# One ScalarE transfer per output tile in place of four from the sync engine, in a linear-attention and two-MoE kernel

## The chip, the cores and the metric

The kernel runs on one core of one Trainium2 chip. The metric is the time of one execution on the device in microseconds (us). The profile is one execution recorded by the hardware profiler; its engines are TensorE (PE, with its weight loads as PEld), VectorE (DVE), ScalarE (ACT), GpSimd (POOL) and the sync engine (SP), which issues transfers and computes nothing.

## The reference

Three stages follow one another. The change lies at the very end of the third.

```python
def _attn_ref(q, k, v, alpha):            # 4 batches, 8 heads, 768 steps, head size 48
    for t in range(S):
        state = alpha[:, :, t, :, None] * state + np.einsum('bhd,bhe->bhde', k[:, :, t], v[:, :, t])
        y[:, :, t] = np.einsum('bhd,bhde->bhe', q[:, :, t], state)

def _moe_ref(x, w_in, w_out, a, b):       # 3072 tokens, 384 -> 2048 -> 384
    h = x @ w_in
    P = a[0] + a[1] * h + a[2] * h**2 + a[3] * h**3
    Q = 1.0 + np.abs(b[0]) * np.abs(h) + np.abs(b[1]) * h**2
    return (P / (Q + 1e-06)) @ w_out

def _moe2_ref(x, w_in, w_out, g_ln):      # 3072 tokens, 384 -> 1024 -> 384
    h = x @ w_in
    solu = h * softmax(h)
    ln = (solu - mean(solu)) / np.sqrt(var(solu) + 1e-06) * g_ln
    return ln @ w_out
```

The result has 3072 rows (batch by step) of 384 float32 numbers.

## The kernel before, in words

The steps are cut into six chunks (NCH) of 128, and a chunk holds 4 batches by 128 steps, which is 512 tokens. Attention and the first MoE run over the chunks together; from about 500 us on only the end of the first MoE and the second MoE are left. The second MoE has 24 tiles `s` of 128 tokens, four to a chunk. The words "up tile" and "down tile" below stand for its two products.

- `n_up` (L696) makes the up product of one tile on PE: 18 matmuls of 512 columns into one of three PSUM buffers.
- `n_soft` and `n_norm` (L713, L730) do the softmax and the normalization, passing the tile between DVE and ACT several times (L722 max, L723 exponential, L726 product, L728 square, L736 and L737, L741), and L743 transposes it in blocks of 32 into a buffer shared by the four tiles of the chunk.
- `n_turn` (L748) runs when all four tiles of a chunk are there: 16 transfers (L753) on SP, each of 32 partitions by 1024 elements, regroup the blocks. A regrouped tile `qq` holds 32 steps of each of the four batches.
- `n_split` (L755) makes a high part on ACT (L758) and a low part (L759) on POOL, or on DVE for tiles 0 and 20. There are three slots of each.
- `n_down` (L762) makes the down product on PE, 24 matmuls of 384 columns into one of two PSUM buffers `op`.
- `n_out` (L773) copies `op` to an SBUF tile `o` on ACT (L776); `o` shares two buffers. Because the partitions of `o` are 4 batches by 32 steps, the tile goes to four separate blocks of the result, each contiguous; the loop at L778 issues one transfer for each from SP (L779), 32 partitions by 384 elements, 48 KB.

The loop at the end of `network` (L915 to L932) writes the tiles out: it splits up to three tiles ahead of the down product, and skips the down product after some up tiles, so that downs run some tiles behind the ups. The last eight down tiles, 16 to 23, come after the last up tile. Each engine executes its own instructions in order. The order on an engine isn't quite that of the program text: the tile framework is opened with `schedule_with_timeline_sim=True` (L1042), and a planner orders the instructions by simulated times, and inserts the waits. SP takes all transfers of the kernel in one such order, the L753 transfers of a later chunk and the L779 stores of earlier tiles among them.

After the stage a flag that was computed earlier decides whether a fallback is run (L1013 to L1016); it is not taken here, but its code holds the same functions.

Of the kernel before, what the change touches and what calls it, by code (L numbers as in the profile page):

```python
# [30 lines left out]
def kernel(  # L31
# [15 lines left out]
    nc = tc.nc  # L47
    nc.scalar.preload_act_table_set("natural_log_exp_and_others")
    B, H, S, D = q.shape
# [103 lines left out]
    def network(fast):  # L153
# [7 lines left out]
        if fast:  # L161
# [7 lines left out]
                out=ident, in_=ident, pattern=[[-1, 128]], compare_op=ALU.not_equal, fill=1.0, base=0, channel_multiplier=1  # L169
# [603 lines left out]
        def n_out(s, op):  # L773
            c, qq = divmod(s, 4)
            o = moe_pool.tile([128, DM], F32, name="o", tag="st", bufs=2)
            nc.scalar.activation(o, op, AF.Copy)  # L776
            to = out.rearrange("(b c q j) d -> c q b j d", b=B, c=NCH, q=4)[c, qq]
            for b in range(B):  # L778
                nc.sync.dma_start(out=to[b], in_=o[32 * b:32 * b + 32])  # L779

        def n_tile(s):
            n_up(s)
# [132 lines left out]
        for s in range(len(EARLY), NS):  # L915
            if s % B == 0 and 1 < s // B + 1 < NCH:
                _run(n_load(s // B + 1))
            n_tile(s)
            if s % B == B - 1:
                n_turn(s // B)  # L920
            while cut < min(done + AHEAD, (s + 1) // B * B):
                n_split(cut)
                cut += 1
            if s not in SKIP:
                n_out(done, n_down(done))
                done += 1
        while done < NS:
            while cut < min(done + AHEAD, NS):
                n_split(cut)
                cut += 1  # L930
            n_out(done, n_down(done))
            done += 1  # L932
# [114 lines left out]
```

## Time and profile before

| | us |
|---|---|
| median of 3 runs | 805.31 (801.63 to 811.93) |
| the profiled execution, its own time | 804.26 |
| its span, first to last instruction | 802.5 |
| mean granted TensorE clock in it | 0.955 of full speed |

The span covers what the engines recorded; 1.76 us of the execution's time lie outside it. Times in the rows below are counted from the start of the span. In a timeline row the first number is the start, the second the duration, both in us; "idle before" in brackets says how long the engine had waited and for what. The SPq rows are the sync engine's issues of transfers, merged where several follow one another.

### The profile page before, as it was taken

What the parts mean: (1) busy time and instruction counts of PE and PEld (TensorE: products, weight loads), DVE (VectorE), ACT (ScalarE), POOL (GpSimd) and SP (SyncE); (2) the same over time, 40 slices, a digit from 0 to 9 for tenths busy, and PEclk for the clock granted to TensorE, in tenths of its full rate; (3) what the DMA queues carried; (4) which work ended last, traced back from release to release, by engine and by line L of the source; (5) the groups of instructions that cost most, each with busy time, mean ns of one, the idle gap of its engine ahead of it and who ended that gap; (6) DMA issues with size and microseconds to landing.
All of it is one profiled execution on the core that took longest, in us unless ns stands there. A gap on an engine that the chain in (4) does not pass through costs nothing. (4 is left out here: it accounts for less than half of the span.)

```text
span 802.5 us, 13911 instructions
## 1 busy us (share of the span) xinstructions
PE 733.8 (91%) x4976; PEld 611.1 (76%) x4976; DVE 641.6 (80%) x1110; ACT 534.4 (67%) x983; POOL 363.8 (45%) x306
## 2 busy tenths in 40 slices
PE   4677787889999989999999999999999999999995
PEld 4565565667787868877777788888888989988994
DVE  6894998998999898979898976567877697877720
ACT  2224756678786878788887879788775555555531
POOL 3254757777654554445454434243242524452331
PEclk9857798999999989999999999999999999999998
DMA  7778229362764476454827160460014454451552
GB/s 170 171 177 245 83 83 235 100 162 79 236 150 149 92 242 137 138 119 141 199 78 176 50 135 14 148 247 0 1 44 111 128 115 109 125 118 48 125 133 57
DMA packets 87279, 101.75 MB, mean 127 GB/s; under 512 B 34464, under 2 KB 63136, under 8 KB 87200
## 3 DMA queue, kind: packets, MB, share of 16 engines
q1 hardware_dynamic: 87200, 100.77, 47.6%
q8 instruction: 41, 0.67, 0.4%
q14 instruction: 38, 0.31, 0.1%
HBM read 60.59 MB, written 27.56 MB: 110 GB/s over the span
## 5 line engine op out<-in xcount | busy, mean ns | idle before, releaser
L583 PE MATMUL hp<-xt,g 128*128 128x512 f32 x864 | 229.0, 408 | 24.5 <-DVE p L614 19.9
L583 PEld LDWEIGHTS hp<-xt,g 128*128 128x128 f32 x864 | 165.3, 195 | 66.8 <-DVE p L614 25.3
L617 POOL TENSOR_TENSOR gl<-p,gh 128x512 fp32r<-128x512 f32 x96 | 130.5, 1359 | 187.3 <-ACT gh L616 114.5
L629 PE MATMUL x2p<-gh,g 128*128 128x512 f32 x576 | 196.5, 397 | 0.2 <-ACT gh L616 0.2
L629 PEld LDWEIGHTS x2p<-gh,g 128*128 128x128 f32 x576 | 109.8, 191 | 25.9 <-issue 0.6
L629 PE MATMUL x2p<-gl,g 128*128 128x512 f32 x288 | 113.6, 394 | 0.3 <-POOL gl L617 0.3
L767 PE MATMUL op<-w2oh,room 128*128 128x384 f32 x384 | 101.8, 339 | 0.2 <-DVEq L1014 0.2
L759 POOL TENSOR_TENSOR room<-room,room 128x1024 fp32r<-128x1024 f32 x22 | 53.7, 2445 | 103.0 <-ACT room L758 92.9
L612 DVE SCALAR_TENSOR_TENSOR w<-w,co,hp 128x512 f32<-128x512 f32 x84 | 62.0, 738 | 43.0 <-ACT hp L611 42.5
L703 PE MATMUL h<-w2ih,x 128*128 128x512 f32 x288 | 90.8, 395 | 0.0
L591 ACT ACTIVATE w<-ah,co 128x512 f32<-128x512 f32 x96 | 69.3, 721 | 7.1 <-DVE hp L613 6.9
L590 ACT ACTIVATE p<-hp,co 128x512 f32<-128x512 f32 x96 | 65.8, 685 | 12.2 <-POOL gl L617 11.7
L609 DVE SCALAR_TENSOR_TENSOR p<-p,co,hp 128x512 f32<-128x512 f32 x84 | 61.8, 735 | 14.1 <-ACT p L590 13.6
L616 ACT ACTIVATE gh<-p 128x512 fp32r<-128x512 f32 x96 | 59.9, 624 | 18.5 <-DVE p L614 8.0
L611 ACT ACTIVATE hp<-ah 128x512 f32<-128x512 f32 x84 | 50.1, 596 | 32.1 <-DVE p L609 31.5
L767 PEld LDWEIGHTS op<-w2oh,room 128*128 128x128 f32 x384 | 70.1, 188 | 1.6 <-DVEq L1014 0.5
L588 ACT ACTIVATE ah<-hp 128x512 f32<-128x512 f32 x96 | 56.5, 589 | 15.6 <-PE hp L583 15.4
L767 PE MATMUL op<-w2ol,room 128*128 128x384 f32 x192 | 65.1, 339 | 0.0
L629 PEld LDWEIGHTS x2p<-gl,g 128*128 128x128 f32 x288 | 54.4, 189 | 12.7 <-POOL gl L617 0.8
L703 PEld LDWEIGHTS h<-w2ih,x 128*128 128x128 f32 x288 | 53.9, 188 | 11.7
L614 DVE SCALAR_TENSOR_TENSOR p<-p,co,hp 128x512 f32<-128x512 f32 x84 | 62.0, 739 | 1.0
L610 ACT ACTIVATE ah<-w,co 128x512 f32<-128x512 f32 x84 | 60.5, 720 | 1.3
(165 smaller groups left out, 1280.4 us busy)
## 6 DMA issues: line engine op xcount, KB each, us to landing
room<-room SPq DMA_DIRECT2D x96, 128.0 KB, 2.3
qk_d<-qk SPq DMA_DIRECT2D x10, 771.0 KB, 4.5
st<-in_moe_w_in_dram SPq DMA_DIRECT2D x15, 512.0 KB, 5.2
st<-in_moe_w_out_dram SPq DMA_DIRECT2D x20, 384.0 KB, 3.8
qks<-qk_d SPq DMA_DIRECT2D x20, 257.0 KB, 5.6
x<-x_d SPq DMA_DIRECT2D x18, 256.0 KB, 3.4
out_dram<-o SPq DMA_DIRECT2D x96, 48.0 KB, 1.6
ra<-in_alpha_dram SPq DMA_DIRECT2D x44, 96.0 KB, 2.8
```

The costliest lines, as they stand in the source:

```text
L583: last["PE", u] = nc.tensor.matmul(hp, lhsT=w[:, kt, 128 * o:128 * o + 128], rhs=xts[c][:, kt, xx, :], start=(kt == 0 and w is hi and xx = ...
L590: nc.scalar.activation(p, hp, AF.Square, bias=co[:, 7:8])
L591: nc.scalar.activation(w, ah, AF.Square, bias=co[:, 6:7])
L609: nc.vector.scalar_tensor_tensor(p, p, a1, hp, ALU.add, ALU.mult)
L610: nc.scalar.activation(ah, w, AF.Ln, bias=rest)
L612: nc.vector.scalar_tensor_tensor(w, w, rest, hp, ALU.add, ALU.mult)
L614: fin[u] = nc.vector.scalar_tensor_tensor(p, p, a0, hp, ALU.add, ALU.mult)
L616: last["ACT", u] = nc.scalar.activation(gh, p, AF.Copy)
L617: last["POOL", u] = nc.gpsimd.tensor_tensor(gl, p, gh[:].bitcast(F32), ALU.subtract)
L629: nc.tensor.matmul(x2ps[c][d], lhsT=w[:, o, 128 * d:128 * d + 128], rhs=gg, start=(f == 0 and w is hi and gg is gh), stop=(f == NF1 - 1 an ...
L703: nc.tensor.matmul(hp[:, 512 * n:512 * n + 512], lhsT=x2s[c][:, kt, x, CH * b:CH * b + CH], rhs=w2[w][:, kt, 512 * n:512 * n + 512], start ...
L767: nc.tensor.matmul(op, lhsT=x[:, 128 * f:128 * f + 128], rhs=w2[w][:, f, :], start=(f == 0 and x is hi and w == "oh"), stop=(f == NF2 - 1 ...
```

## The change

The loop of four transfers over the batches is replaced by one transfer of the whole tile, 128 partitions by 384 elements (192 KB), with a destination of three dimensions (4 batches, 32 steps, 384). It is issued by ACT, the engine that makes `o`.

```diff
         def n_out(s, op):
             c, qq = divmod(s, 4)
             o = moe_pool.tile([128, DM], F32, name="o", tag="st", bufs=2)
             nc.scalar.activation(o, op, AF.Copy)
             to = out.rearrange("(b c q j) d -> c q b j d", b=B, c=NCH, q=4)[c, qq]
-            for b in range(B):
-                nc.sync.dma_start(out=to[b], in_=o[32 * b:32 * b + 32])
+            nc.scalar.dma_start(out=to, in_=o)
```

## Rows read from the trace of the kernel before

**Rows 1.** Page, busy time of each engine, with share of the span and instructions

```profile
PE 733.8 (91%) x4976; PEld 611.1 (76%) x4976; DVE 641.6 (80%) x1110; ACT 534.4 (67%) x983; POOL 363.8 (45%) x306
```

**Rows 2.** Stretches: length, then busy PE, PEld, DVE, ACT, POOL; clock, DMA share, GB/s

```profile
625.00:766.00 141.00, 141.00 (x708) 127.84 (x707) 107.25 (x220) 79.04 (x157) 54.98 (x27) 1.00 0.42 106
766.00:793.00 27.00, 26.69 (x149) 25.78 (x147) 3.76 (x6) 7.26 (x12) 7.18 (x4) 1.00 0.53 125
793.00:803.00 10.00, 0.00 (x0) 0.00 (x0) 0.00 (x0) 0.43 (x1) 0.00 (x0) 0.60 0.11 26
```

**Rows 3.** Waits from 755 us on: us in total, times, longest

```profile
ACT o L776 <- DMA out_dram<-o: 1.8, 2, 1.5
PEld op L767 <- DVEq L1014: 0.5, 1, 0.5
PEld op L767 <- ACT o L776: 0.3, 1, 0.3
```

**Rows 4.** Timeline of 762 to 786 us, without PE

```profile
763.43 0.47 ACT L776 ACTIVATE o<-op 128x384 f32<-128x384 f32 x1
...
763.93 5.13 SPq L779 DMA_DIRECT2D out_dram<-o  x8
...
764.12 1.15 ACT L728 ACTIVATE jk<-room,sm 128x1024 bf16<-128x1024 f32 x1 [0.22 <-DVE sm L727]
...
767.48 1.25 DVE L743 STREAM_TRANSPOSE room<-room 128x1024 f32<-128x1024 f32 x1
769.17 11.06 SPq L753 DMA_DIRECT2D room<-room  x16
...
773.41 1.06 ACT L758 ACTIVATE room<-room 128x1024 fp32r<-128x1024 f32 x1 [1.85 <-DMA room<-room]
774.51 1.22 DVE L759 TENSOR_TENSOR room<-room,room 128x1024 fp32r<-128x1024 f32 x1 [5.78 <-ACT room L758]
775.36 0.49 ACT L776 ACTIVATE o<-op 128x384 f32<-128x384 f32 x1 [0.88 <-PE op L767]
776.01 1.06 ACT L758 ACTIVATE room<-room 128x1024 fp32r<-128x1024 f32 x1 [0.17 <-DMA room<-room]
777.15 2.39 POOL L759 TENSOR_TENSOR room<-room,room 128x1024 fp32r<-128x1024 f32 x1 [11.15 <-ACT room L758]
...
780.33 5.63 SPq L779 DMA_DIRECT2D out_dram<-o  x12
```

**Rows 5.** Timeline of PE's weight loads where they waited

```profile
775.78 0.30 PEld L767 LDWEIGHTS op<-w2oh,room 128*128 128x128 f32 x2 [0.48 <-DVEq L1014]
...
784.11 0.19 PEld L767 LDWEIGHTS op<-w2oh,room 128*128 128x128 f32 x1 [0.26 <-ACT o L776]
```

**Rows 6.** SP's issues of three lines: duration min/median/max in ns, first and last start

```profile
L779 SPq DMA_DIRECT2D out_dram<-o x96: 314/419/1634, 631.4 to 796.0; - x96
...
L638 SPq DMA_DIRECT2D x_d<-x2e x12: 320/376/932, 198.2 to 624.4; - x12
...
L541 SPq DMA_DIRECT2D w2o_d<-st x8: 524/525/525, 306.5 to 430.0; - x8
```

**Rows 7.** Page, transfers: count, KB each, median us from issue to landing

```profile
room<-room SPq DMA_DIRECT2D x96, 128.0 KB, 2.3
...
out_dram<-o SPq DMA_DIRECT2D x96, 48.0 KB, 1.6
...
x_d<-x2e SPq DMA_DIRECT2D x6, 256.0 KB, 3.3
```

**Rows 8.** Timeline of ACT and SP at the end, and one 1 us stretch

```profile
792.94 0.49 ACT L776 ACTIVATE o<-op 128x384 f32<-128x384 f32 x1 [3.75 <-PEq L1014]
793.45 2.92 SPq L779 DMA_DIRECT2D out_dram<-o  x4
...
795.96 0.42 SPq L779 DMA_DIRECT2D out_dram<-o  x1
...
794.00:795.00 1.00, 0.00 (x0) 0.00 (x0) 0.00 (x0) 0.00 (x0) 0.00 (x0) 0.97 0.46 114
```

## The prediction, made before the run

> **What bounds the kernel now.** I read the views from the whole to the place of the change. The page's busy times come first: PE leads with 91% of the span, and DVE with 80% and ACT with 67% come behind [rows 1]. A share over the whole span says little about one stage, so the view of stretches is next. The stores start at 631 us [rows 6], so only the stretches from 625 us on matter. There PE is busy in all of 141 us up to 766, and in 26.69 of the 27 us up to 793, at the full granted clock; ACT is busy in 79.04 and 7.26 us of the same stretches, so 61.96 + 19.74 = 81.7 us of ACT are free [rows 2]. After 793 us only the last copy and the last stores are left, with the way out of the program: 10 us in which no engine computes anything else.
>
> Then the waits: in the tail PE's weight loads wait twice in all, 0.5 us for DVE and 0.3 us for the copy of an output tile [rows 3]. The stage is thus bound by PE, with two small holes and a short end. The timeline says where the holes come from. The last up tile leaves PE at about 758 us, and PE then lives on the eight down tiles that are left. The first four of them (16 to 19) are all it has until the last chunk is regrouped and split. That chain runs: square of tile 23 on ACT at 764.12, its transpose on DVE ending at 767.48 + 1.25 = 768.73, 16 transfers on SP from 769.17, the split of tile 20 on ACT at 773.41 and on DVE until 774.51 + 1.22 = 775.73 [rows 4]; PE picks up at 775.78, 0.48 us late [rows 5]. The second hole, 0.26 us at 784.11 [rows 5], is PE waiting for a free `op`.
>
> **What the change removes.** On SP, 96 issues at a median of 0.419 us go: 40 us [rows 6]. SP is not the bound, so this counts only where SP holds something up, and that is in three places.
>
> First, the stores of tiles 16 and 17 occupy SP on and off for 5.13 us from 763.93, to 769.06, and the transfers of the last chunk are issued at 769.17 although the transpose was done at 768.73 [rows 4]. SP free, they could go out up to 0.4 us earlier, on the chain that ends in the 0.48 us hole.
>
> Second, the stores of tile 18 stand behind the 16 regrouping transfers, and go out only from 780.33 [rows 4]. That is why two copies wait 1.8 us for a free `o` [rows 3]. The first of these, of tile 20, is 0.26 us late, and PE's second hole is just as long. Issued by ACT right behind its copy, the store of tile 18 goes out at about 771.6 and the wait is gone: -0.3 us.
>
> Third, the end. The last copy ends at 792.94 + 0.49 = 793.43; four issues take 2.92 us, the last starts at 795.96 [rows 8] and lands 1.6 us later [rows 7], at 797.56. With one transfer, the issue starts at about 793.5. Its landing time is not in the trace for 192 KB: 128 KB land in 2.3 us and 256 KB in 3.3 us [rows 7]. I take the middle, 2.8 us, which gives 796.3 and -1.3 us. The bounds are 2.3 us (-1.8) and, for a store that uses fewer engines, 4.6 us (+0.5), which is worked out below. The exit behind it, 802.5 - 797.6 = 4.9 us, stays.
>
> **What it adds.** ACT gets 24 issues, each waiting for its own copy. That wait is small: the copy of tile 16 ends at 763.90 and SP issues at 763.93 [rows 4]. The issue's price on ACT isn't in the trace, since ACT issues no transfer there. Stores of 128 partitions cost SP 0.376 us and 0.525 us at the median; the stores of `o` range from 0.314 to 1.634 us [rows 6]. It can't be below nothing: an issue is one more instruction in an in-order queue. I take 0.5 us, with 0.3 and 1.6 us as ends. So 24 x 0.53 = 13 us, 39 us at worst, against 81.7 us free. As a sum it is hidden by PE's work; what counts is what stands behind an issue on the chain of the last chunk.
>
> Two instructions do. The square of tile 23 starts at 764.12, 0.22 us after the copy of tile 16 ended [rows 4]. An issue of 0.5 us between them ends at 764.43 and moves the square by 0.3 us (1.4 us at the upper end). That eats the 0.4 us that SP gives back on the same chain, so I put the two together at nothing, with -0.4 and +1.0 as ends. The split of tile 21 starts at 776.01, after the copy of tile 19 ended at 775.85. The issue moves it by 0.4 us, and its low part on POOL, done at 777.15 + 2.39 = 779.54 [rows 4], by as much. PE needs it two matmuls into that down tile. Down tile 20 starts at 775.78 [rows 5] and PE's 149 matmuls in 27 us [rows 2] make some 0.18 us each, so its 24 end at about 780.1 and the low part is needed at 780.4. The slip fits in the 0.9 us of slack; at 1.6 us it would cost 0.7. Up to 766 us no split came late, since PE has no idle time there [rows 2]; up tiles that are ready fill PE between the chunks. This covers the other 16 or so issues; if it were gone, each would cost its 0.5 us, 8 us in all.
>
> **The sum.** -0.3 (second hole) - 1.3 (end) + 0 (chain) = -1.6 us, against the profiled execution's 804.26 (span 802.5 and 1.76 around it): 802.7. The median of the runs, 805.31, lies 1.05 us above that execution, so the forecast is 805.31 - 1.6 = 803.7 us. That is 0.2%; about 2% (16 us) is what a measurement of this kernel can tell from no change.
>
> **Rivals.**
>
> Narrow store. One transfer may be spread over fewer DMA engines than the four. Its destination's outermost dimension has 4 entries, where each of the four transfers had 32 rows. In the stretch of 794 to 795 us the stores moved 114 GB/s at a DMA share of 0.46 [rows 8], so 16 engines make some 248 GB/s and four some 62. A 48 KB store takes 1.6 us [rows 7], of which 0.2 move data at 248 GB/s, leaving 1.4 fixed. On four engines 192 KB take 1.4 + 3.2 = 4.6 us. The end then comes at 798.1, +0.5, and the whole at +0.2: 805.5 us. For it speaks only the shape; against it nothing in the trace, which has no transfer of such a shape. The two buffers of `o` would still be free in time, since two down tiles of PE last 2 x 24 x 0.18 = 8.6 us.
>
> The Trainium skill, "DMA: Bandwidth & Descriptors", section "Why a DMA increments its semaphore by 16 and not by 1", says in substance that a transfer uses the largest number of engines, up to 16, that divides the slowest dimension on both sides. For 4 on one side and 128 on the other that is four, and by that rule this rival would be the outcome. No run here shows it yet.
>
> ACT held up (the slower side). An issue on ACT costs as much as SP's slowest, 1.6 us. The place is the last chunk: the square of tile 23 slips 1.4 us, the whole chain with it, 1.0 us after SP's gain; tile 21's split then slips by the issue as well, 0.7 us; with the end at its upper bound of +0.5, and the issue's own excess of 1.1 us perhaps delaying the landing, +3.3 us: 808.6. It decides from an issue of about 0.8 us, where the slip exceeds what SP gives back. For it: the last four issues did contain one of that length (they take 2.92 us, where four medians make 1.7 [rows 6, 8]). Against it: the median is a quarter of it.
>
> Planner rearranges. The order on ACT and PE in the tail comes from simulated times; with a store on ACT, copies and splits may change places, and PE could lose a few tenths up to a tile (24 x 0.18 = 4.3 us) at the chunk's border: up to 808. For it: the two holes show how tight the last chunk is. Against: an order that keeps PE fed had over 4 us of spare cover elsewhere.
>
> Nothing at all. The stores were hidden but for the end, and the exit may wait for something else than their landing: 805.3.
>
> **How the numbers follow.** The forecast has 0.45; the narrow store 0.28; ACT held up 0.1; the planner 0.09; nothing 0.08. All of them lie within 803 to 809 us, inside 2%. What is beyond comes from the runs themselves, which spread over 10 us with the same kernel (801.63 to 811.93), and from an order that I can't see. So the range is 799 to 812: the lowest run less the largest gain (0.4 + 0.3 + 1.8 = 2.5), the highest run as it is. Faster by over 2%, 0.02; within 2%, 0.94; slower by over 2%, 0.04, the last from the two rivals on the slower side, if they came several times over.
>
> **What would show it.** Right: ACT's issues at about 0.5 us; no copy waiting for a store; the regrouping transfers of the last chunk issued right after the transpose; PE without the 0.26 us hole; the last store issued within 0.1 us of the copy's end and landed 2.8 us later. Wrong: a landing near 4.6 us (narrow store), issues over 0.8 us with PE waiting for splits (ACT held up), or another order of PE's tiles. The forecast as a whole is wrong if PE in the tail waits for more than a few microseconds, or if the exit after the landing is not 4.9 us.

## The result: 1.1% slower, and the profile after

| | before | after |
|---|---|---|
| median of 20 runs | 805.2 us | 814.63 us (811.12 to 817.62) |
| ratio of the two | | 1.0112, 95% interval 1.0093 to 1.0131 |
| the profiled execution, its span | 804.26, 802.5 us | 817.17, 815.5 us |

The forecast of 803.7 us (799 to 812) was wrong: the kernel got 9.4 us slower, which is clear of the noise, since the interval of the ratio does not reach 1, though under 2%. One of the 20 runs of before took 2469.6 us and is left out of the ratio.

The page after shows PE's busy time up by 5 us only, with a span 13 us longer, and a second queue for ScalarE's stores. In the queue rows the columns are packets, MB and the share of the time of sixteen DMA engines.

```profile
PE 739.0 (91%) x4976; PEld 614.4 (75%) x4976; DVE 644.2 (79%) x1110; ACT 535.2 (66%) x983; POOL 363.0 (45%) x306
...
q1 hardware_dynamic: 82592, 96.04, 44.9%
q10 hardware_dynamic: 3168, 4.72, 2.1%
```

3168 packets for 24 stores are 132 each: the 128 rows of 1536 bytes and four more, of 4 bytes each. That fits a store spread over four engines with one small packet from each; the DMA share while a store is alone in flight, shown below, confirms the four. The same count is used for the other shapes: 128 plus the number of engines.

Four stages of the tail account for the 13.0 us between the two profiles. Each is the difference of the same step in the two timelines.

- PE's first up tile of the tail starts at 598.55 us instead of 595.86: +2.7. PE's clock in the first 100 us was granted at 0.73 instead of 0.76 in this execution; this is before any store, and not put down to the change.
- The last up tile ends at 762.90 instead of 758.15: +4.75, of which 2.7 are from above, so +2.0. PE waits here, too: 1.2 us for a copy of an output tile (L776) and 0.2 us for L726.
- From there to the end of the last copy it is 805.96 - 762.90 = 43.1 us instead of 793.43 - 758.15 = 35.3: +7.8. Both hold the same eight down tiles.
- From the last copy to the end of the span, 9.54 us instead of 9.07: +0.5.

So most of the loss is behind the last up tile. The waits of PE (engine, line and releaser; us in total, times, longest) from 600 us on; the last row is the only one of the same view before:

```profile
PE op L767 <- ACT room L758: 3.9, 1, 3.9
PE op L767 <- POOL room L759: 1.4, 1, 1.4
PE op L767 <- ACT o L776: 1.2, 1, 1.2
PE op L767 <- DVE room L759: 0.6, 1, 0.6
...
PE op L767 <- DVEq L1014: 0.2, 1, 0.2
```

And the timeline of the last chunk without PE, the counterpart of [rows 4]; the merged SPq row is followed by two single issues out of the sixteen, and then by PE's weight load that waited:

```profile
768.62 0.55 ACTq L778 DMA_DIRECT2D out_dram<-o  x1
769.22 1.15 ACT L728 ACTIVATE jk<-room,sm 128x1024 bf16<-128x1024 f32 x1 [0.62 <-ACT o L776]
...
772.04 0.55 ACTq L778 DMA_DIRECT2D out_dram<-o  x1
772.58 1.25 DVE L743 STREAM_TRANSPOSE room<-room 128x1024 f32<-128x1024 f32 x1
773.90 15.50 SPq L753 DMA_DIRECT2D room<-room  x16
...
776.28 0.55 ACTq L778 DMA_DIRECT2D out_dram<-o  x1
...
777.24 2.60 SPq L753 DMA_DIRECT2D room<-room  x1
778.71 1.06 ACT L758 ACTIVATE room<-room 128x1024 fp32r<-128x1024 f32 x1 [2.45 <-DMA room<-room]
...
780.53 0.55 ACTq L778 DMA_DIRECT2D out_dram<-o  x1
...
781.90 2.44 SPq L753 DMA_DIRECT2D room<-room  x1
...
787.99 1.06 ACT L758 ACTIVATE room<-room 128x1024 fp32r<-128x1024 f32 x1 [7.49 <-DMA room<-room]
...
789.09 0.29 PEld L767 LDWEIGHTS op<-w2oh,room 128*128 128x128 f32 x1 [4.19 <-ACT room L758]
```

The sixteen regrouping transfers take SP 15.50 us instead of 11.06. Two of the issues take 2.60 and 2.44 us, and they begin 0.96 and 1.37 us after ScalarE began to issue a store (776.28, 780.53). The split of tile 20 starts 4.8 us after the first regrouping issue instead of 4.2, and that of tile 21 comes 9.3 us after that of tile 20, where it had been 2.6. PE has run out of work by then and waits 4.19 us.

Stretches of 1 us show what the DMA engines did (length, PE, PEld, DVE, ACT, POOL, PE's clock, DMA share, GB/s); the last two rows split the first stretch by queue, ScalarE's (q10) and SP's (q1):

```profile
779.00:780.00 1.00, 1.00 (x7) 0.83 (x6) 0.20 (x1) 0.77 (x1) 0.00 (x0) 1.00 0.19 49
783.00:784.00 1.00, 1.00 (x7) 1.00 (x6) 0.00 (x0) 0.00 (x0) 0.00 (x0) 1.00 0.20 65
790.00:791.00 1.00, 0.10 (x1) 0.00 (x0) 0.00 (x0) 0.81 (x2) 1.00 (x1) 0.50 0.69 148
809.00:810.00 1.00, 0.00 (x0) 0.00 (x0) 0.00 (x0) 0.00 (x0) 0.00 (x0) 0.50 0.26 97
...
q10 hardware_dynamic: 32, 0.05, 19.1%
q1 hardware_dynamic: 5, 0.00, 0.2%
```

At 809 us only the last store is in flight: a share of 0.26 is four engines of sixteen, moving 97 GB/s. In the two long issues of SP the share is 0.19 and 0.20. From 779 to 780 us it is ScalarE's store alone that moves data, 0.05 MB; SP's queue shows five packets and no bytes to speak of. So while SP stands still, about a fifth of the engines work and the rest move nothing. The third row shows a cost that follows from the stall: after 4.19 us in which PE waited, its clock was granted at 0.5, that is 1.2 of 2.4 GHz, until 794.3. The eleven matmuls of that stretch took 0.34 us each instead of 0.18, some 1.8 us in all.

The forecast's step on the issue was right: ScalarE's issues take 547 ns at the median. What they did to the chain was small, too: the square of tile 23 waited 0.62 us for one.

```profile
L778 ACTq DMA_DIRECT2D out_dram<-o x24: 547/547/1148, 634.1 to 806.0; - x24
...
L753 SPq DMA_DIRECT2D room<-room x96: 507/590/2605, 616.2 to 788.8; - x96
```

### The profile page after: what moved, and what is told of

The parts are those of the page before. It is cut to its first block, busy times and chain, and to the rows that moved or that the text cites. A ratio compares the mean times of both kernels' runs of the same rounds, so it can differ in the third digit from the quotient of the medians.

```text
span 815.5 us, 13792 instructions
## 1 busy us (share of the span) xinstructions
PE 739.0 (91%) x4976; PEld 614.4 (75%) x4976; DVE 644.2 (79%) x1110; ACT 535.2 (66%) x983; POOL 363.0 (45%) x306
## 3 DMA queue, kind: packets, MB, share of 16 engines
q10 hardware_dynamic: 3168, 4.72, 2.1%
## 5 line engine op out<-in xcount | busy, mean ns | idle before, releaser
L767 PE MATMUL op<-w2oh,room 128*128 128x384 f32 x384 | 103.5, 344 | 7.2 <-ACT room L758 3.9
```

The source lines that it names most:

```text
L767: nc.tensor.matmul(op, lhsT=x[:, 128 * f:128 * f + 128], rhs=w2[w][:, f, :], start=(f == 0 and x is hi and w == "oh"), stop=(f == NF2 - 1 ...
```

## Experiments

The theory: the store runs on four engines, 48 KB on each, and the regrouping transfers, which need all sixteen, get done no sooner than these four. The rivals: ScalarE's queue beside SP's, or the issues on ScalarE, whatever the shape; or the new order of instructions that the planner made when the store moved.

**Four kernels on the engine and the shape.** In two of them the tokens of a tile are interleaved, with the result the same, so that the destination's outermost dimension has 32 entries:

```diff
 n_norm:
-                out=_view(T, 32 * b, [[128, NF2], [NF2 * 128, 4], [1, 32]]),
+                out=_view(T, b, [[128, NF2], [NF2 * 128, 4], [B, 32]]),
 n_out:
-            to = out.rearrange("(b c q j) d -> c q b j d", b=B, c=NCH, q=4)[c, qq]
+            to = out.rearrange("(b c q j) d -> c q j b d", b=B, c=NCH, q=4)[c, qq]
```

> One store of the whole tile from ScalarE as in the changed kernel, but with the tokens of a tile interleaved (step outermost, batch inside), so that the destination's outermost dimension has 32 entries instead of 4; the bytes, the row length, the engine and the order of the instructions are those of the changed kernel, and the block transpose of L743 writes with a step of four. Narrow store (theory): the store in the changed kernel runs on four DMA engines (132 packets each, against 128 rows) and holds them for some 3 us, and the 16 regrouping transfers of a chunk, which need all sixteen, wait for them; with 32 it is spread wide, SP's issue of the last 16 regrouping transfers goes back from 15.5 to about 11 us, PE's 4 us hole is gone, and the time is 802 to 806 us. Rival, ScalarE's queue or the issues on ScalarE themselves: nothing changes, 813 to 816. Rival, the planner's new order: the order is the same here, so 813 to 816 as well.

Measured: 815.39 us, ratio to before 1.0147 (1.011 to 1.0184), where the theory had 802 to 806. By the time alone it would fall. The trace says that the experiment was not the one intended: the block transpose, 1.24 us in the changed kernel, took 2.05 us with writes four elements apart, on DVE, which works on the chain of every chunk.

```profile
L743 DVE STREAM_TRANSPOSE room<-room x24: 1999/2048/2078, 565.2 to 776.0; 128x1024 f32<-128x1024 f32 x24
```

The 32-entry kernel further below keeps the order and the engine and leaves the transpose alone, and it takes 804.2 us, so the slow transpose is what this one paid for. The part that the theory speaks of did change as expected: the last regrouping block took 10.31 us.

```profile
778.15 10.31 SPq L753 DMA_DIRECT2D room<-room  x16
```

> The interleaved, wide single store, issued by the sync engine. Narrow store (theory): nothing holds the regrouping transfers, and SP has 24 issues in place of 96: 802 to 805 us, the least of this call or level with the one from ScalarE. Rival, that any single store of 192 KB gets in the way: as slow as the narrow one from the sync engine.

Measured: 819.12 us, 1.0187 (1.0149 to 1.0225), with the same slow transpose. It tells nothing of the store.

The third undoes half of the change:

```diff
-            nc.scalar.dma_start(out=to, in_=o)
+            nc.sync.dma_start(out=to, in_=o)
```

> The changed kernel's one store with a destination of 4 x 32 x 384, but issued by the sync engine again. Narrow store (theory): the four engines are held from this queue as well, and the regrouping transfers stand behind it in the same queue, so the time stays above that of before: 808 to 818 us. Rival, issues on ScalarE or its queue: those are gone, 802 to 806.

Measured: 805.54 us, 1.0028 (0.9995 to 1.0061). As the rival said, and not the 808 to 818 of the theory: the narrow store from the sync engine does hardly any harm. So narrowness alone isn't the cost; where the store stands among SP's transfers must matter with it. In this trace the last regrouping block takes 11.44 us, about as before. What the narrow store delays here is ScalarE: behind the block its copies wait 6.3 us in all for a store to free `o`, and PE waits 1.6 us for a copy.

The fourth undoes the other half, with four issues per tile on ScalarE:

```diff
-            nc.scalar.dma_start(out=to, in_=o)
+            for b in range(B):
+                nc.scalar.dma_start(out=to[b], in_=o[32 * b:32 * b + 32])
```

> The four stores of before, 32 partitions each, but issued by ScalarE. Narrow store (theory): each is spread over sixteen engines, so the regrouping transfers go through; what is left is four issues of 0.4 us on ScalarE per tile, 24 x 1.7 = 40 us of it, partly on the chain of a chunk: 804 to 812 us. Rival, the queue of ScalarE beside that of SP: as slow as the changed kernel or slower, 814 to 820, with the long issues of SP still there.

Measured: 808.99 us, 1.007 (1.0048 to 1.0093), between the two, as the theory has it. PE waits 2.2 us for a split, and the last regrouping block takes 12.38 us. The planner's order is another one here, and ScalarE has four issues per tile, so the 0.7% isn't settled between the two.

**The number of engines as a dose.** The next three keep ScalarE and the number of bytes; only the destination's walk differs. In the traces the order of the instructions is that of the changed kernel, on DVE, ACT, POOL and SP throughout and on PE in the whole second MoE. The rows of a tile land in exchanged places of the result.

```diff
 32 entries, the same rows of the result:
-            to = out.rearrange("(b c q j) d -> c q b j d", b=B, c=NCH, q=4)[c, qq]
+            to = out.rearrange("(b c q j) d -> c q j b d", b=B, c=NCH, q=4)[c, qq]
 8 entries, one block of 128 rows (2 entries: w=2):
+            to = out[128 * s:128 * s + 128].rearrange("(u w) d -> w u d", w=8)
```

> The changed kernel with one thing altered: the destination of the store is walked step first, batch inside, so its outermost dimension has 32 entries instead of 4 (the rows of a tile then land in exchanged places; the same bytes in the same rows of the result are written). All instructions, their order and the engine are the changed kernel's, and L743 is untouched, unlike in the interleaved version, where it took 2.05 us instead of 1.25. Narrow store (theory): the regrouping block of the last chunk goes from 15.5 back to some 11 us, PE's stalls in the tail from 7.2 to under 3 us, and the time is 804 to 809 us. Rival, the queue of ScalarE beside SP's or the issues on ScalarE: unchanged, 813 to 816. Rival, the planner's order: unchanged too, since the order is the same.

Measured: 804.2 us, 0.9995 (0.9971 to 1.002), the low end of what the theory had. All of the loss is gone with the order, the engine and the queue as they were. 144 packets per store are 128 and sixteen engines; the block takes 10.86 us, and PE waits 0.6 us in the tail:

```profile
q10 hardware_dynamic: 3456, 4.72, 1.7%
...
766.91 10.86 SPq L753 DMA_DIRECT2D room<-room  x16
...
PE op L767 <- DVEq L1013: 0.6, 1, 0.6
```

> The changed kernel with a store whose destination's outermost dimension has 8 entries (8 x 16 x 384; each tile is written as a block of 128 rows of the result, rows exchanged); the order of all instructions is the changed kernel's. Narrow store (theory): half the changed kernel's hold of a DMA engine, 1.6 instead of 3.2 us of data each, so a time between that of the 32-entry store and that of the changed kernel: 807 to 812 us, and 128 + 8 = 136 packets per store on ScalarE's queue. Rivals (queue, issues, order): 813 to 816 as with 4.

Measured: 804.19 us, 0.9985 (0.9962 to 1.0009), better than expected: at eight engines (136 packets) the block is longer, 12.41 us, but the work that PE has in hand still covers it.

```profile
771.68 12.41 SPq L753 DMA_DIRECT2D room<-room  x16
...
PE op L767 <- DVEq L1013: 0.6, 1, 0.6
PE op L767 <- POOL room L759: 0.2, 1, 0.2
```

> The same with 2 entries (2 x 64 x 384): two engines, 96 KB and some 6.3 us each. Narrow store (theory): twice the changed kernel's hold, each regrouping block that meets a store waits up to 6 us: 825 to 845 us, with 130 packets per store. Rivals (queue, issues, order): 813 to 816.

Measured: 819.79 us, 1.0196 (1.0155 to 1.0236). Slower than with four, but by 5 us, where I had expected 10 or more. With two engines (3120 packets, 130 each) the block takes 18.33 us, and one wait of PE alone is 7.2 us:

```profile
q10 hardware_dynamic: 3120, 4.72, 1.7%
...
773.52 18.33 SPq L753 DMA_DIRECT2D room<-room  x16
...
PE op L767 <- ACT room L758: 7.2, 1, 7.2
```

So the last block goes 10.86, 12.41, 15.50, 18.33 us with 16, 8, 4 and 2 engines, and the time 804.2, 804.2, 814.6, 819.8: the block grows at each step, and the time only once PE's cover is used up. The shares bear out the counts: with such a store alone in flight the DMA share is 0.90 of sixteen engines (792.9 to 793.3 us of its trace), 0.52 (799.0 to 799.5), 0.26 (above) and 0.13 (806 to 807). Of the last step's 5 us much is not the block: from the last copy to the end of the span it is 12.3 us with two engines and 9.5 with four.

These traces also settle the +2.0 us before the last up tile. From the first up matmul of the second MoE to the last it takes 230.4 us before and with 32 and 8 entries, 232.5 with 4 and 233.0 with 2, in the same order. So these 2 us, too, belong to the narrow store. In the changed kernel a store goes out at 651.89 and a regrouping block begins at 651.91; the first split behind it comes 7.8 us after the block's begin, where it is 4.9 with 32 entries.

> The 32-entry store, issued by the sync engine: against the 4-entry store from the sync engine (805.5, same order) it tells what narrowness costs where the store stands in the same queue as the regrouping transfers. Narrow store (theory): a little less than that, 802 to 805, since there most stores go out between the regrouping blocks. Rival, that only the queue of ScalarE matters: the same 805.5 within 1.

```diff
 against the one narrow store from the sync engine:
-            to = out.rearrange("(b c q j) d -> c q b j d", b=B, c=NCH, q=4)[c, qq]
+            to = out.rearrange("(b c q j) d -> c q j b d", b=B, c=NCH, q=4)[c, qq]
```

Measured: 802.04 us, 0.9971 (0.9942 to 0.9999), the rows exchanged as above. On SP the step from four engines to sixteen takes the ratio from 1.0028 to 0.9971, about half as much as on ScalarE (1.0112 to 0.9995); each ratio is known to some 0.2 to 0.3%. The loss is of another kind, too. The last block hardly differs (11.14 us against 11.44); what the wide store takes away is the wait of the copies for `o` (none is left in the tail) and 1.5 us between the last copy and the end of the span (7.8 against 9.3 us).

**Where the harm is done.** In this one only tiles 17, 18 and 19 are stored as in the changed kernel; the other 21 have the wide store with exchanged rows.

```diff
+            dims = "b j" if s in (17, 18, 19) else "j b"
+            to = out.rearrange(f"(b c q j) d -> c q {dims} d", b=B, c=NCH, q=4)[c, qq]
```

> The 32-entry store from ScalarE for all tiles but 17, 18 and 19, which are stored as in the changed kernel (4 entries, four engines). These three are issued at 772.0, 776.3 and 780.5 us of the changed kernel's profile, about the last chunk's regrouping (773.9 to 789.4); the instructions and their order are the changed kernel's. Narrow store at the last chunk's border (theory): most of the loss comes back with three narrow stores of 24, the 7 to 8 us that PE lost after the last up tile: 809 to 813 us, with the last regrouping block at some 15 us. Rival, that the loss is spread over all 24 stores: 10.4 x 3 / 24 = 1.3 us, 805 to 806.

Measured: 813.12 us, 1.0087 (1.0057 to 1.0117). Three stores of 24 bring back most of the loss (1.0112 with all), and with it the long block and the waits in the last chunk. From the first up matmul to the last it takes 230.4 us here, as before; what the other stores cost ahead of the last chunk is gone.

```profile
771.25 15.32 SPq L753 DMA_DIRECT2D room<-room  x16
...
PE op L767 <- ACT room L758: 3.6, 1, 3.6
PE op L767 <- POOL room L759: 1.8, 1, 1.8
PE op L767 <- DVE room L759: 0.6, 1, 0.6
```

**Looking for a version that beats both.** Three kernels with the right result try to keep one wide store. The first two change the order of tokens where it should cost least: the copies of L637 write four batches of 32 steps for each up tile, and the output tile becomes one block of 128 rows.

```diff
 m_down:
-                        nc.scalar.activation(e[:, d], x2ps[c][d0 + d], AF.Copy, scale=back if fast else 1.0)
+                        nc.scalar.activation(
+                            _view(e[:, d], 0, [[32, B], [CH, 4], [1, 32]]), _view(x2ps[c][d0 + d][:], 0, [[CH, B], [32, 4], [1, 32]]),
+                            AF.Copy, scale=back if fast else 1.0,
+                        )
 n_out:
-            to = out.rearrange("(b c q j) d -> c q b j d", b=B, c=NCH, q=4)[c, qq]
+            to = out[S * qq + CH * c:S * qq + CH * c + CH]
```

> The same with the store issued by ScalarE. By the wide store alone: 803 to 806 us, as the 32-entry store from ScalarE (804.2). Rival, the planner's order as above: 800 to 812.

("The same" refers to the version from the sync engine, which follows.) Measured: 803.53 us, 0.9982 (0.9958 to 1.0006). The copies cost what they did (694 ns), the tail has no other wait of PE than 0.6 us, and the loss is gone with the store still on ScalarE. It doesn't beat the kernel before by more than can be measured.

```profile
PE op L770 <- DVEq L1016: 0.6, 1, 0.6
```

> A version that makes the store wide with the right result: the copies of L637 write the tokens of a chunk in another order (four batches of 32 steps per up tile), so that a down tile holds 128 steps of one batch and its 128 rows are one block of the result; one store per tile, from the sync engine. If a wide store is all that is needed and L637 costs no more (0.70 us each, 18 of them): 801 to 804 us, as the 32-entry store from the sync engine (802.0). Rival, that the planner's order, which changes from the first MoE on since L637's copies have another shape, costs or gives some: 800 to 812.

Measured: 807.34 us, 1.0034 (1.0008 to 1.006), slower than the wide store alone would have it and inside the rival's range. Against the 32-entry kernel from the sync engine, ACT and DVE have another order from 664 us on; in the tail PE waits 2.2 us for a split. Which instruction's place costs that wasn't tried.

The third reads the regrouped tile with a step in the split, and stores with 32 entries from the sync engine (not shown in the cut):

```diff
 n_split:
+            L = _view(L, 0, [[128, NF2], [1, 32], [32, B]])
+            hi4, lo4 = (_view(t, 0, [[128, NF2], [4, 32], [1, B]]) for t in (hi, lo))
-            nc.scalar.activation(hi, L, AF.Copy)
-            (nc.vector if s in FASTS else nc.gpsimd).tensor_tensor(lo, L, hi.bitcast(F32), ALU.subtract)
+            nc.scalar.activation(hi4, L, AF.Copy)
+            (nc.vector if s in FASTS else nc.gpsimd).tensor_tensor(lo4, L, hi4.bitcast(F32), ALU.subtract)
```

> Another right version of the wide store from the sync engine: the split (L758 on ScalarE, L759 on GpSimd) reads the regrouped tile with batch inside step, so that the rows of the output tile are step by batch and the destination's outermost dimension has 32 entries. If the reads with a step of 32 elements cost nothing: 801 to 804 us. Rival, that they slow L758 (1.06 us) or L759 (2.40 us) as the step of four slowed L743 on VectorE: GpSimd has to make one tile in 8.4 us, so up to twice the time would still hide but for the last chunk, where three of them follow one another: 804 to 812.

Measured: 820.46 us, 1.0209 (1.0177 to 1.024), as its rival said and worse: the split on ACT, which took 1.06 us, took twice that (L760 there), and PE waits 7.5 us in all for copies, which stand behind the splits on ACT.

```profile
L760 ACT ACTIVATE room<-room x24: 1974/2126/2170, 617.8 to 797.5; 128x1024 fp32r<-128x1024 f32 x24
```

## Why the prediction was wrong, step by step

**The bound** was read rightly: the tail belongs to PE, and its weak place is the border of the last chunk, where PE lives on the down tiles that are left. That is where the time was lost.

**The end** held in the main. I had 2.8 us for a wide store and 4.6 for a narrow one. In the changed kernel the last store is issued at 805.99 and its last packet ends at 810.24; in the 32-entry kernel it is 791.54 and 794.36. The narrow store's +0.5 at the end is what the profile shows; the wide store's -1.3 is -0.8 in the 32-entry kernel, and up to that size in the other wide ones.

**The price on ScalarE** held: 0.55 us per issue against 0.5, and a slip of 0.6 us on the square of tile 23. With a wide store and the same 24 issues in the same order the time was 804.2 us, so the issues cost nothing that can be measured. The forecast of 803.7 can't be told from that. Its terms are there only in part: in the 32-entry kernel the time from the last up tile to the last copy is 0.4 us longer than before, not 0.3 shorter.

**The step that failed** is the price of the narrow store. I gave it as a rival, 0.28, at 805.5 us, and worked out only how long the store itself takes, at the end of the kernel; elsewhere I asked only whether "the two buffers of `o` would still be free in time". I did not ask who else needs the engines that it holds, and so the sum has the chain of the last chunk at 0, with -0.4 and +1.0 as ends, and the regrouping transfers on it at the length that they had. They use all sixteen engines (sixteen 4-byte packets each in the trace, and a DMA share of 0.96 from 774 to 775 us in the 32-entry kernel), and PE waits for them in the last chunk. The size that I gave the store, 3.2 us of data on four engines, was right: the packets of an undisturbed one run for 3.1 us (798.70 to 801.82). What it does to a transfer that meets it is what the chain lacked: two issues of SP took 2.60 and 2.44 us in place of 0.59 and the block 15.5 us in place of 11.06, the split of tile 21 came 9.3 us behind that of tile 20 in place of 2.6, and PE lost 5.9 us to waits where it had lost 0.2, and some 1.8 us to the halved clock behind them, nearly all of the 7.8. That three such stores bring back 1.0087 of 1.0112 shows the place. Of the signs that I had set, PE waiting for more than a few microseconds in the tail is the one that came.

**The second failure** is a sign in the sum. I counted it a gain (-0.3 us) that the store of tile 18 would no longer stand behind the sixteen regrouping transfers on SP, but go out right behind its copy [rows 4]. Standing there had cost a wait of 0.26 us; it had also kept the stores out of the regrouping. With ScalarE issuing, three stores fall into it. The narrow store issued by SP, 805.54 us, bears this out: the same shape, but the block takes 11.44 us, and only the wait for `o` grows. Both together, narrow and free to collide, make the loss.

**The rule that I weighed**, of the Trainium skill ("DMA: Bandwidth & Descriptors", section "Why a DMA increments its semaphore by 16 and not by 1"), was right in every shape tried: 2, 4, 8 and 32 entries against 128 partitions gave 2, 4, 8 and 16 engines by the packet counts and the DMA shares. A rule that the trace can't contradict deserved more than 0.28. The same page of the Trainium skill says in "Issuing engines are not separate DMA queues" that transfers of all issuers share the same sixteen engines; the profile agrees, with the stalls of SP's issues behind ScalarE's stores.

**The slower rivals.** "ACT held up" did not happen. "Planner rearranges" did in part: the orders of ACT and DVE did change from 636 us on, but the 32-entry kernel, in the changed kernel's order, has 804.2 us, so this order costs nothing measurable. Two smaller losses, both in other orders, stay unexplained: the four wide stores per tile from ScalarE, 808.99 us, and the regrouped tokens with the store from SP, 807.34 us.

What stays open is why SP's issue itself stands still. That regrouping data hardly moves meanwhile, although most engines are idle, is measured (779 to 780 us, by queue); that the parts of a regrouping transfer for the four busy engines pile up behind the store and hold back the rest is inferred from it.

## What to carry to other kernels

Merging transfers can narrow them: compare the outermost dimension of both sides before and after, and count packets to see how many DMA engines a transfer really has. Price a slow transfer by what else needs its engines at that moment and who waits for that, not by its own landing. An in-order queue that delays a harmless transfer may be what keeps it from colliding with an urgent one, so ask of every transfer that is moved what it will now run beside.

## What the runs showed that I had not expected

- Access with a step has its price on three engines here: the block transpose with writes four elements apart took 2.05 us instead of 1.24 on DVE, the split with reads 32 elements apart 2.13 instead of 1.06 on ACT, and its low part 2.98 instead of 2.40 on POOL. The copy of L637 with runs of 32 contiguous elements cost nothing (694 ns both ways).
- The loss does not go in proportion: with eight engines the regrouping block is 14% longer than with sixteen (12.41 against 10.86 us), and the time is the same.
- A stall of 4.19 us in PE cost some 1.8 us more, since the granted clock behind it was 0.5 from 789.1 to 794.3 us.
